# Products of ones on TensorE in a kernel of attention, eight experts and a feed-forward stage

## The chip, the cores and the metric

The kernel runs on one core of a Trainium2 chip. The metric is the device time of one execution in microseconds (us), from a few runs, of which the median is given. One further execution was profiled; its times are the rows shown below. The engines are TensorE (PE; its weight loads PEld), VectorE (DVE), ScalarE (ACT), GpSimd (POOL) and SyncE (SP), which issues DMAs. Each works through its own instructions in their order and waits for others by semaphores.

## The reference, cut to what matters

```python
scores = q @ k.T / sqrt(64) + cum[i] - cum[j]        # 32 heads, 576 rows, causal; cum = cumsum(log f)
x = softmax(scores) @ v                              # as 2304 tokens of 512
logits = normed(x) @ normed(expert_emb).T / tau      # 8 experts
e = argmax(logits); gate = softmax(logits)[e]
x = gate * (relu(x @ w1[e]) @ w2[e])                 # 512 -> 1024 -> 512, one expert for each token
h = x @ w_in
out = softplus(h) @ w_out                            # 512 -> 2048 -> 512
```

## The kernel before, in words

Nearly every product is split into a high and a low part so that float32 accuracy is kept: three products (high by high, high by low, low by high) stand where one would do.

**Attention** goes over 16 pairs of heads; a pair has five units (four blocks of 128 query rows, and one with the last 64 rows of both heads). One loop over n (80 units and some lags) writes the order of the work out by hand. In step n the letters of the string `NSTXVPXLXGLFAL` call in turn: N the normalising of an older unit, S the scores of unit n, X its softmax (DVE takes the maximum at L306, ACT the exponential), V the power of two that scales v (ACT squares at L249, POOL's `vmb` at L251, a product with ones on TensorE at L254, DVE's `vbits`), P the transposes of the next pair's q and k rows (`prep`, L207) and their split (ACT's copy, then POOL at L217 and L218), T and L the transposes of the probabilities and their split, A the product with v, F the transposes of finished rows (L454), G the logits. The loads of q, k, v and of the decay rows `cb` are issued on SP; `cb` can only be read back after `cum` has been computed and stored. PSUM has three banks for scores (tag s), three for transposes (T) and two for the products with v (A3, A2).

**Routing.** After the last logits DVE picks the expert of each row, TensorE counts ranks by products with a triangle of ones, and DVE computes counts, slots and tables: `pm(V)` (L781) makes, between other steps, the one-hot tables `pms[t]`, each 128x128, for 12 of the 20 row blocks (ACT makes the first eight). TensorE sums 20 products of them to `pid` (L835), from which comes the list of rows `gidx`. ACT meanwhile rounds the first expert's weights (L745, and at L1336 four tiles of its second matrix).

**Experts.** Nine phases, of three, two or one slot of 128 rows. POOL gathers a slot's rows (L1061), TensorE transposes them (L1085, for the first phase two at a time), ACT and DVE split them (L1086, L1087). Then eight groups of products `h` (L1149; in the first phase 12 products of 384 columns each), whose results leave through three PSUM banks: ACT's ReLU (`hh`, L1154) and DVE's rest (`hl`, L1155). Then the products `y` (L1129). In the first phase DVE splits four tiles of the second weight matrix (L1029) ahead of the first `hl`, and the gates (L861 to L870, root and exponential on ACT) are computed behind the first group. The weights of the next phases are loaded through four buffers (`raw`, SP), rounded on ACT and split on DVE into a ring of eight pairs of tiles, which TensorE frees.

**Feed-forward.** Five chunks of rows; products and softplus alternate until the end.

`g.onesm` is a tile of 128x128 ones in bfloat16, used later for sums over rows; POOL sets it at L82.

Of the kernel before, what the change touches and what calls it, by code (L numbers as in the profile page):

```python
# [9 lines left out]
F32 = mybir.dt.float32  # L10
# [14 lines left out]
B, H, S, D = 4, 8, 576, 64  # L25
N = B * S
DM = H * D
# [28 lines left out]
@with_exitstack  # L56
def body(ctx, tc, q, k, v, f, emb, tau, w1, w2, win, wout, out):
    nc = tc.nc
    const = ctx.enter_context(tc.tile_pool(name="const", bufs=1))
    dram = ctx.enter_context(tc.tile_pool(name="dram", bufs=1, space=DRAM))  # L60
    stage = ctx.enter_context(tc.tile_pool(name="stage", bufs=4))
    g = Shared()
    g.stage = stage
    g.xd = dram.tile([N, DM], F32, name="xd")
    g.gd = dram.tile([B * SB, 1], F32, name="gd")
    g.yd = nc.dram_tensor("yd", [N + 128 * NSLOT, WROW], F32, kind="Internal").ap()
    g.ydv = dram_disjoint_views(g.yd, NSLOT + 1)
    g.ncum = dram.tile([B * H, S], F32, name="ncum")

    nc.scalar.preload_act_table_set(LN_EXP)  # L70
    g.ident = const.tile([128, 128], F32, name="ident")
    make_identity(nc, g.ident)
    g.gidx = const.tile([128, NMAIN], I32, name="gidx")
    g.sidx = const.tile([128, NMAIN], I32, name="sidx")
    g.ids = const.tile([1, 3 * NG + 4], I32, name="ids")
    g.pv = const.tile([128, 3, NMAIN], F32, name="pv")
    g.gsl = const.tile([128, NMAIN], F32, name="gsl")
    g.tok = const.tile([128, NMAIN], F32, name="tok")
    g.grow = const.tile([128, NMAIN], I32, name="grow")
    g.oidx = const.tile([128, N // 128], I32, name="oidx")  # L80
    g.onesm = const.tile([128, 128], BF16, name="onesm")
    nc.gpsimd.memset(g.onesm, 1.0)  # L82
    g.ysq = const.tile([128, NSLOT], F32, name="ysq")
    nc.gpsimd.memset(g.ysq, 0.0)
    g.wsq = const.tile([128, 2, 8], F32, name="wsq")
    g.junk = const.tile([128, 1024], BF16, name="junk")
    g.lt = const.tile([128, T, E], F32, name="lt")
    g.mx = const.tile([128, T, 1], F32, name="mx")
    g.nrm = const.tile([128, T], F32, name="nrm")
    g.gs = const.tile([128, T], F32, name="gs")  # L90
    g.nr = const.tile([128, T, 1], F32, name="nr")

    const.tile([128, 40], F32, name="pad")
    g.const = const
    g.pre = []
    with ExitStack() as acc:
        ps_s = attention(tc, g, acc, q, k, v, f, emb, tau, w1)
        g.home = ctx.enter_context(tc.tile_pool(name="home", bufs=16, reuse_waits="tile"))
        ring = ctx.enter_context(tc.tile_pool(name="ring", bufs=8, reuse_waits="tile"))

        def wtile(dt=F32R, n=1024):
            return (ring.tile([128, n], dt, name="wh", tag="wh"), ring.tile([128, n], dt, name="wl", tag="wl"))

        g.wtile = wtile
        g.w2a = w2[0]
        with ExitStack() as rtx:
            route(tc, g, rtx.enter_context(tc.tile_pool(name="r_p", bufs=1)), ps_s)
    experts(tc, g, w1, w2, win, wout, out)


class Shared:
    pass


def attention(tc, g, acc, q, k, v, f, emb, tau, w1):
    nc = tc.nc
    ident, xd, ncum, nrm = g.ident, g.xd, g.ncum, g.nrm
    with ExitStack() as ctx:
# [5 lines left out]
        ps_s = acc.enter_context(tc.tile_pool(name="a_ps", bufs=3, space=PSUM))  # L124
        ps_t = acc.enter_context(tc.tile_pool(name="a_pt", bufs=3, space=PSUM))
        ps_a = acc.enter_context(tc.tile_pool(name="a_pa", bufs=1, space=PSUM))
# [21 lines left out]
        def load(i, what):  # L148
            r = loaded.setdefault(i, {})
            for nm in what:  # L150
                if nm == "v":
                    r[nm] = rows_in(vbuf[i % 3], v, i)
                elif nm == "c":
                    bh = 2 * i
                    c = r[nm] = ld.tile([128, 3, S], F32, name="cb", tag="cb")
                    for h in range(2):
                        nc.sync.dma_start(c[:, h], ncum[bh + h:bh + h + 1, :].to_broadcast([128, S]))
                        nc.sync.dma_start(c[64 * h:64 * h + 64, 2], ncum[bh + h:bh + h + 1, :].to_broadcast([64, S]))
                else:
                    r[nm] = rows_in(ld.tile([128, 5, 2, D], F32, name=nm + "t", tag=nm + "t"), q if nm == "q" else k, i)  # L160
# [373 lines left out]
        La, Lb, Lc, Lf, Lg = [2, 3, 4, 5, 8]  # L534
        seq = [(i, u) for i in range(NPAIR) for u in order]
        n_all = len(seq)
        prep(0, 0)
        nc.scalar.dma_start(ncum, cum)
        prep(0, 1)
        prep(0, 2)  # L540
        load(0, "c")
        load(1, "kvc")
        vs0 = scale(0)
# [23 lines left out]
        for n in range(n_all + Lg + 1):  # L567
            now = at_lag(0)
            if now and now[1] == order[0 if now[0] else 3] and now[0] + 2 < NPAIR:
                load(now[0] + 2, "qkcv")  # L570
            pt_ = ptrans(*at_lag(La)) if at_lag(La) else iter(())
            sf = soft(*now) if now else iter(())
            for c in "NSTXVPXLXGLFAL":
                if c == "S" and now:
                    scores(*now)
                if c == "N" and at_lag(Lc):
                    norm(*at_lag(Lc))
                if c in "TL":
                    next(pt_, None)
                if c == "X":  # L580
                    next(sf, None)
                if c == "A" and at_lag(Lb):
                    av(*at_lag(Lb))
                if c == "F" and at_lag(Lf):
                    for runs in ready(*at_lag(Lf)):
                        finish1(at_lag(Lf)[0], runs)
                if c == "G" and at_lag(Lg):
                    i, u = at_lag(Lg)
                    for runs in ready(i, u):
                        finish2(i, runs)  # L590
                    if u == order[-1] and i % 4 == 3:
                        pick(i // 4)
                        norms(i // 4)
                if c == "V" and now and now[0] + 1 < NPAIR:
                    steps = [order[x] for x in ([1, 2, 4] if now[0] else [2, 3, 4])]
                    if now[1] == steps[0]:
                        vsg = scale(now[0] + 1)
                    if now[1] in steps:
                        next(vsg, None)
                    if now[1] == order[4]:  # L600
                        vprep(now[0] + 1)
                if c == "P" and now:
                    for j, at_ in enumerate([0, 1, 3]):
                        if now[1] == order[at_] and now[0] + 1 < NPAIR:
                            prep(now[0] + 1, j)
            for x in (pt_, sf):
                for _ in x:
                    pass
            if n == 0:
                for _ in vs0:  # L610
                    pass
                vprep(0)
            if n == 6:
                gate_consts()
                pick_consts()
            if n == n_all - 20:
                for c in range(4):
                    r = g.stage.tile([128, 1024], F32, name="raw", tag="raw")
                    nc.sync.dma_start(r, w1[0, 128 * c:128 * c + 128, :])
                    g.pre.append(r)  # L620
            if n == n_all:
                rk = rank_start(tc, g, ps_s, oh)
# [107 lines left out]
def route(tc, g, p, psp):  # L730
    nc, lo, n, code = tc.nc, g.lo, g.n, g.code
# [8 lines left out]
    start = tl([128, T, NMAIN], "start", BF16)  # L740
# [17 lines left out]
    pms = [p.tile([128, 8, 128], BF16, name="pm", tag="pm", bufs=3) for _ in range(3)]  # L758
    first8 = pms[0]
    pms = [pms[t // 8][:, t % 8] for t in range(T)]  # L760
    made = iter(range(8, T))

    away = tl([128, 8, 128], "away", BF16)
# [13 lines left out]
    def pm(eng, k=1):  # L777
        for _ in range(k):
            t = next(made, None)
            if t is not None:  # L780
                eng.tensor_scalar(pms[t], g.iof, lo[:, t:t + 1], None, op0=ALU.is_equal)  # L781

    cnt = tl([128, 3, E], "cnt")
    r = tl([128, E], "r")
# [30 lines left out]
    x = 0  # L815
# [160 lines left out]
def experts(tc, g, w1, w2, win, wout, out):  # L976
    nc = tc.nc
# [5 lines left out]
    with ExitStack() as both, ExitStack() as ctx:  # L983
# [103 lines left out]
                nc.vector.tensor_sub(lo[:, cs, a], t, hi[:, cs, a].bitcast(F32))  # L1087

        def xprep(ph):
            for a in range(len(XG[ph])):  # L1090
                xslot(ph, a)

        def xnext(ph, turn):
            if ph + 1 < n_ph and turn < len(XG[ph + 1]):
# [236 lines left out]

        conv = Conv(tc, g, win, wout)
        xgather(0)
        for r in g.raw2:
            w = tuple(t.rearrange("p (a d) -> p a d", a=2) for t in g.wtile())
            nc.scalar.activation(w[0], r, ACTF.Copy)  # L1336
            g.first.append(w)
        TW = [(spare([128, 1024], F32R), spare([128, 1024], F32R)) for _ in range(4)]
        TR = [spare([128, 1024], F32) for _ in range(2)]
# [314 lines left out]
```

## Time and profile before

| | |
|---|---|
| median of 3 runs | 901.26 us (901.11 to 901.83) |
| profiled execution | 901.85 us, of which the span from first to last instruction is 900.1 us |
| mean granted TensorE clock | 0.983 |
| busy: PE, DVE, ACT, POOL | 857.4, 700.3, 565.7, 379.8 us |
| shares of the chain that ended last: PE, DVE, ACT, DMA | 71%, 11%, 5%, 4% |

How to read it: a timeline row has the start in us from the span's beginning, a duration in us, the engine, the line of the kernel, the operation with output<-input, sizes and the number of instructions merged, and in brackets how long the engine had been idle and what released it. [...] The chain follows the last instruction back to what released it at each step. The modelled end of a product includes its way through the array, so the distance of two starts is its cost, not the duration of one.

### The profile page before, as it was taken

To read this page: it belongs to the slowest core of one execution; us is meant where nothing else is said; L and a number is where in the kernel's file an instruction comes from. 1 tells how busy PE (TensorE), PEld (TensorE's weight loads), DVE (VectorE), ACT (ScalarE), POOL (GpSimd) and SP (SyncE) were. 2 spreads that over 40 slices of the span, in tenths; PEclk is the share of its full clock that TensorE was granted. 3 is DMA by queue.
4 is the path that set the end of the run, shared out by engine and by line. 5 is a ranking of instruction groups with operands and counts; after the bars stand their busy time and mean duration, and the time that the engine had idled before them with its cause. 6 is when DMAs were issued, how large, how long until landed. Compare 5 with 4: busy or idle time off the path is not lost.

```text
span 900.1 us, 17321 instructions
## 1 busy us (share of the span) xinstructions
PE 857.4 (95%) x6298; PEld 595.5 (66%) x6298; DVE 700.3 (78%) x1541; ACT 565.7 (63%) x1052; POOL 379.8 (42%) x524
## 2 busy tenths in 40 slices
PE   5999999999649999999899999999999999999998
PEld 4788787888549998998799744444444444664443
DVE  4888888888678777777689878778878787777775
ACT  5778879787554666674756775755445545566453
POOL 6678777767242222432513143325323322434221
PEclk9999999999759999999999999999999999999999
DMA  8967566681335888888868110102000100100001
GB/s 172 192 163 167 136 159 158 145 234 37 118 101 180 275 285 265 276 269 273 289 212 295 52 67 1 37 13 71 25 0 14 58 1 1 59 1 25 1 1 47
DMA packets 102816, 109.74 MB, mean 122 GB/s; under 512 B 62949, under 2 KB 72185, under 8 KB 102721
## 3 DMA queue, kind: packets, MB, share of 16 engines
q1 hardware_dynamic: 97282, 93.49, 36.9%
q0 software_dynamic: 5152, 14.87, 4.6%
q8 instruction: 52, 0.85, 0.4%
q14 instruction: 44, 0.35, 0.1%
q10 hardware_dynamic: 286, 0.17, 0.1%
HBM read 93.31 MB, written 15.20 MB: 121 GB/s over the span
## 4 chain that ended last, share of the span: by engine, by line
PE 71%; DVE 11%; ACT 5%; DMA 4%; POOL 4%; issue 4%; SPq 1%; DVEq 0%; POOLq 0%; ACTq 0%
PE h L1520 14%; PE h L1149 12%; PE y L1565 11%; PE y L1129 9%; PE t L1565 4%; PE s L284 4%; PE av L407 2%; PE pt L355 2%; POOL e L1534 2%; DVE r L1531 2%; DMA raw<-in_moe_w_dram 2%; DVE e L1545 2%; PE tps L207 1%; DVE wl L1041 1%; PE av L408 1%
## 5 line engine op out<-in xcount | busy, mean ns | idle before, releaser
L1534 POOL TENSOR_TENSOR e<-u,e 128x512 f32<-128x512 f32 (+1 forms) x80 | 105.2, 1316 | 240.4 <-DVE u L1533 237.1
L1530 ACT ACTIVATE e<-h,s_h 128x512 f32<-128x512 f32 (+1 forms) x80 | 51.2, 640 | 116.8 <-PE h L1520 116.8
L1565 PE MATMUL y<-dw,gh 128*128 128x512 f16 x448 | 111.4, 379 | 0.6 <-ACT ob L1573 0.6
L1552 DVE SCALAR_TENSOR_TENSOR gl<-e,s_gup,gh 128x512 f16<-128x512 f32 (+1 forms) x80 | 94.5, 1181 | 8.5 <-ACT gh L1550 8.1
L1565 PEld LDWEIGHTS <-gh 128*128 128x128 f16 x576 | 56.3, 98 | 65.2 <-issue 0.9
L1041 DVE TENSOR_TENSOR wl<-raw,wh 128x1024 fp32r<-128x1024 f32 x64 | 77.8, 1223 | 19.4 <-ACT wh L1040 19.3
L1149 PE MATMUL h<-xl,wh 128*128 128x384 f32 (+1 forms) x256 | 79.6, 311 | 1.7 <-DVE xl L1087 1.7
L1149 PE MATMUL h<-xh,wl 128*128 128x384 f32 (+1 forms) x256 | 79.7, 311 | 0.7 <-DVE wl L1041 0.5
L1040 ACT ACTIVATE wh<-raw 128x1024 fp32r<-128x1024 f32 x64 | 67.1, 1056 | 20.6 <-DMA raw<-in_moe_w_dram 19.2
L1149 PE MATMUL h<-xh,wh 128*128 128x384 f32 (+1 forms) x256 | 79.9, 312 | 0.0
L335 DVE SCALAR_TENSOR_TENSOR pts<-pt,pts 128x512 f16<-128x512 f32 (+3 forms) x128 | 69.9, 567 | 12.8 <-ACT pts L332 12.0
L1531 DVE TENSOR_SCALAR r<-h,s_h 128x512 f32<-128x512 f32 (+1 forms) x80 | 55.6, 695 | 31.1 <-ACT e L1530 31.1
L1520 PEld LDWEIGHTS <-wh 128*128 128x128 f16 x480 | 46.9, 98 | 46.7 <-issue 0.3
L1520 PEld LDWEIGHTS <-wl 128*128 128x128 f16 x480 | 47.0, 98 | 46.4
L1550 ACT ACTIVATE gh<-e,s_gup 128x512 f16<-128x512 f32 (+1 forms) x80 | 53.6, 671 | 36.1 <-DVE e L1546 36.1
L332 ACT ACTIVATE pts<-pt 128x512 f16<-128x512 f32 (+3 forms) x128 | 58.5, 495 | 22.7 <-PE pt L355 11.0
L309 ACT ACTIVATE p<-sm,mx 128x512 f32<-128x512 f32 (+3 forms) x128 | 67.8, 558 | 2.1 <-DVE mx L306 1.8
L1545 DVE TENSOR_TENSOR e<-r,e 128x512 f32<-128x512 f32 (+1 forms) x80 | 50.4, 630 | 22.4 <-POOL e L1534 22.4
L1129 PE MATMUL y<-wh,hh 128*128 128x512 f32 x168 | 67.8, 404 | 0.0
L306 DVE CUSTOM_DVE_ANT_0 sm<-s,cb 128x512 f32<-128x512 f32 (+3 forms) x128 | 58.3, 484 | 11.4 <-PE s L286 6.5
L1129 PE MATMUL y<-wl,hh 128*128 128x512 f32 x168 | 65.7, 391 | 0.0
L1520 PE MATMUL h<-yth,wh 128*128 128x512 f16 x192 | 64.9, 379 | 0.0
(344 smaller groups left out, 2421.5 us busy)
## 6 DMA issues: line engine op xcount, KB each, us to landing
raw<-in_moe_w_dram SPq DMA_DIRECT2D x68, 512.0 KB, 4.6
cb<-ncum SPq DMA_DIRECT2D x32, 288.0 KB, 4.7
raw<-in_moe_w_in_dram SPq DMA_DIRECT2D x16, 512.0 KB, 5.2
raw<-in_moe_w_out_dram SPq DMA_DIRECT2D x16, 512.0 KB, 5.2
yg<-yd SPq DMA_DIRECT2D x18, 264.0 KB, 2.8
cb<-ncum SPq DMA_DIRECT2D x32, 144.0 KB, 5.1
qt<-in_q_dram SPq DMA_DIRECT2D x32, 128.0 KB, 2.9
kt<-in_k_dram SPq DMA_DIRECT2D x32, 128.0 KB, 2.8
```

Source lines behind the costliest of these rows:

```text
L309: nc.scalar.activation(p[:, 0:n], s[:, 0:n], ACTF.Exp, scale=-1.0, bias=m)
L335: nc.vector.scalar_tensor_tensor(lo, ps, UP, hi, op0=ALU.mult, op1=ALU.subtract)
L1040: nc.scalar.activation(hi, r, ACTF.Copy)
L1041: nc.vector.tensor_sub(lo, r, hi.bitcast(F32))
L1129: nc.tensor.matmul(py[a], x[:, 128 * a:128 * a + 128], w[:, fb % 2], start=(fb == 0 and m == 0 and w is wh), stop=(fb == 7 and m == 1))
L1149: nc.tensor.matmul(pl, x[:, fs], y[:, c], start=(c == 0 and m == 0), stop=(c == 3 and m == 2))
L1520: nc.tensor.matmul(pl, w[:, fs], x[:, d], start=(d == 0 and m == 0), stop=(d == 3 and m == 2))
L1531: nc.vector.tensor_scalar(r, pl, back, 0.0, op0=ALU.mult, op1=ALU.max)
L1534: nc.gpsimd.tensor_sub(e, u, e)
L1545: nc.vector.tensor_sub(d, r, d)
L1552: nc.vector.scalar_tensor_tensor(gl, d, s, gh, op0=ALU.mult, op1=ALU.subtract)
L1565: nc.tensor.matmul(PO[c][a], x, w, start=(fb == 0 and m == 0 and w is wh), stop=(fb == FB - 1 and m == 1))
```

## The change

A helper issues products of a tile with another that write into a PSUM tile which nobody reads. It is called before the first transposes, between them, after the first unit's scaling, inside step 1 and after the last product with v, in the routing behind each of ten one-hot tables (with the table as weights), behind each of four rounded weight tiles (with the tile itself, 512 columns) and behind each of the first phase's three slots. The memset of `onesm` moves from POOL to DVE. The output is not touched.

```diff
@@ -79,7 +79,7 @@
     g.grow = const.tile([128, NMAIN], I32, name="grow")
     g.oidx = const.tile([128, N // 128], I32, name="oidx")
     g.onesm = const.tile([128, 128], BF16, name="onesm")
-    nc.gpsimd.memset(g.onesm, 1.0)
+    nc.vector.memset(g.onesm, 1.0)
     g.ysq = const.tile([128, NSLOT], F32, name="ysq")
     nc.gpsimd.memset(g.ysq, 0.0)
     g.wsq = const.tile([128, 2, 8], F32, name="wsq")
@@ -110,6 +110,11 @@
 
 class Shared:
     pass
+
+
+def spin(nc, ps, x, y, n):
+    for _ in range(n):
+        nc.tensor.matmul(ps[0:x.shape[-1], 0:y.shape[-1]], x, y, start=True, stop=True)
 
 
 def attention(tc, g, acc, q, k, v, f, emb, tau, w1):
@@ -534,10 +539,14 @@
         La, Lb, Lc, Lf, Lg = [2, 3, 4, 5, 8]
         seq = [(i, u) for i in range(NPAIR) for u in order]
         n_all = len(seq)
+        idle = ps_a.tile([128, 4 * (D + 1)], F32, name="av", tag="A2")
+        spin(nc, idle, g.onesm, g.onesm, 30)
         prep(0, 0)
         nc.scalar.dma_start(ncum, cum)
+        spin(nc, idle, g.onesm, g.onesm, 4)
         prep(0, 1)
         prep(0, 2)
+        spin(nc, idle, g.onesm, g.onesm, 3)
         load(0, "c")
         load(1, "kvc")
         vs0 = scale(0)
@@ -599,6 +608,8 @@
                         next(vsg, None)
                     if now[1] == order[4]:
                         vprep(now[0] + 1)
+                if c == "P" and n == 1:
+                    spin(nc, idle, g.onesm, g.onesm, 20)
                 if c == "P" and now:
                     for j, at_ in enumerate([0, 1, 3]):
                         if now[1] == order[at_] and now[0] + 1 < NPAIR:
@@ -610,6 +621,10 @@
                 for _ in vs0:
                     pass
                 vprep(0)
+                spin(nc, idle, g.onesm, g.onesm, 20)
+            if n == n_all + Lb - 1:
+                g.idle = ps_s.tile([128, 512], F32, name="idle", tag="s")
+                spin(nc, g.idle, g.onesm, g.onesm, 20)
             if n == 6:
                 gate_consts()
                 pick_consts()
@@ -758,6 +773,7 @@
     pms = [p.tile([128, 8, 128], BF16, name="pm", tag="pm", bufs=3) for _ in range(3)]
     first8 = pms[0]
     pms = [pms[t // 8][:, t % 8] for t in range(T)]
+    spin(nc, g.idle, g.onesm, g.onesm, 12)
     made = iter(range(8, T))
 
     away = tl([128, 8, 128], "away", BF16)
@@ -779,6 +795,8 @@
             t = next(made, None)
             if t is not None:
                 eng.tensor_scalar(pms[t], g.iof, lo[:, t:t + 1], None, op0=ALU.is_equal)
+                if k == 1:
+                    spin(nc, g.idle, pms[t], g.onesm, 3)
 
     cnt = tl([128, 3, E], "cnt")
     r = tl([128, E], "r")
@@ -1087,8 +1105,11 @@
                 nc.vector.tensor_sub(lo[:, cs, a], t, hi[:, cs, a].bitcast(F32))
 
         def xprep(ph):
+            idle = ps_y.tile([128, DM], F32, name="y", tag="y") if ph == 0 else None
             for a in range(len(XG[ph])):
                 xslot(ph, a)
+                if ph == 0:
+                    spin(nc, idle, g.onesm, g.onesm, 6)
 
         def xnext(ph, turn):
             if ph + 1 < n_ph and turn < len(XG[ph + 1]):
@@ -1331,9 +1352,11 @@
 
         conv = Conv(tc, g, win, wout)
         xgather(0)
+        idle = ps_y.tile([128, DM], F32, name="y", tag="y")
         for r in g.raw2:
             w = tuple(t.rearrange("p (a d) -> p a d", a=2) for t in g.wtile())
             nc.scalar.activation(w[0], r, ACTF.Copy)
+            spin(nc, idle, w[0][:, 0, 0:128], w[0][:, 0], 3)
             g.first.append(w)
         TW = [(spare([128, 1024], F32R), spare([128, 1024], F32R)) for _ in range(4)]
         TR = [spare([128, 1024], F32) for _ in range(2)]
```

## Rows read from the trace of the kernel before

**Rows 1.** The page: the granted clock in 40 slices of 22.5 us, in tenths.

```profile
PEclk9999999999759999999999999999999999999999
```

**Rows 2.** Windows: stretch, length, PE busy (instructions), granted clock, DMA share, GB/s.

```profile
...
237.00:238.00 1.00, 0.00 (x0) 0.90 0.00 0
...
268.00:269.00 1.00, 1.00 (x6) 0.74 0.97 381
...
```

**Rows 3.** The chain that ended last, from the third slot's rows on: start, us, what.

```profile
261.24 0.68 PE t L1085 x2
...
262.83 0.70 PE t L1085 x2
...
263.99 10.74 PE h L1149 x48
...
283.32 2.09 PE y L1129 x9
...
318.47 4.32 DMA raw<-in_moe_w_dram
```

**Rows 4.** Timeline of PE at the first loads.

```profile
4.47 1.09 PE L207 MATMUL tps<-ident,qt 128*128 128x128 f32 x4 [4.47 <-DMA qt<-in_q_dram]
...
17.25 1.09 PE L207 MATMUL tps<-ident,kt 128*128 128x128 f32 x4 [2.20 <-DMA kt<-in_k_dram]
...
27.76 0.60 PE L207 MATMUL tps<-ident,qt 128*128 128x128 f32 x4
```

**Rows 5.** Timeline of PE in the first phase, around the rise of the clock.

```profile
267.50 0.52 PE L1149 MATMUL h<-xl,wh 128*128 128x384 f32 x1
267.82 0.52 PE L1149 MATMUL h<-xh,wl 128*128 128x384 f32 x1
...
269.02 0.34 PE L1149 MATMUL h<-xl,wh 128*128 128x384 f32 x1
269.20 0.33 PE L1149 MATMUL h<-xh,wl 128*128 128x384 f32 x1
```

**Rows 6.** Timeline of POOL and DVE at the first loads.

```profile
1.26 0.19 POOL L82 MEMSET onesm<- 128x128 bf16 x1
...
13.07 0.69 DVE L306 CUSTOM_DVE_ANT_0 sm<-s,cb 128x512 f32<-128x512 f32 x1 [2.13 <-DMA cb<-ncum]
...
15.09 0.62 POOL L217 TENSOR_SCALAR qhi<-qraw 128x512 fp32r<-128x512 f32 x1 [4.79 <-ACT qraw L216]
...
21.55 1.28 POOL L218 TENSOR_TENSOR klo<-kraw,khi 128x512 fp32r<-128x512 f32 x1
...
23.15 0.19 POOL L251 TENSOR_SCALAR vmb<-vm 128x1 bf16<-128x1 f32 x1 [0.32 <-ACT vs L249]
```

**Rows 7.** Timeline of PE at the end of attention.

```profile
238.15 0.66 PE L454 MATMUL xt<-ident,xb 128*128 128x128 f32 x2 [1.56 <-DVE xb L429]
```

**Rows 8.** Timeline of DVE and PE in the routing.

```profile
247.45 0.25 DVE L781 TENSOR_SCALAR pm<-iof,lo 128x128 bf16<-128x128 bf16 x1
...
250.48 0.24 DVE L781 TENSOR_SCALAR pm<-iof,lo 128x128 bf16<-128x128 bf16 x1
...
252.00 1.23 PE L835 MATMUL pid<-rhs,pm 128*128 128x63 bf16 x20 [6.60 <-DVE rhs L829]
```

**Rows 9.** Timeline of ACT and PE between routing and first phase.

```profile
252.35 3.88 ACT L1336 ACTIVATE wh<-dw 128x1024 fp32r<-128x1024 f32 x4
...
258.47 1.09 PE L1085 MATMUL t<-ident,xg 128*128 128x128 f32 x4 [5.25 <-DMA xg<-xd,gidx]
```

**Rows 10.** Timeline of DVE in the first phase.

```profile
264.74 4.67 DVE L1029 TENSOR_TENSOR wl<-dw,wh 128x1024 fp32r<-128x1024 f32 x4
269.33 0.55 DVE L1155 SCALAR_TENSOR_TENSOR hl<-h,hh 128x384 fp32r<-128x384 f32 x1
270.48 0.18 DVE L863 TENSOR_SCALAR nr<-nr 128x20 f32<-128x20 f32 x1 [0.60 <-ACT nr L861]
...
280.01 1.01 DVE L1155 SCALAR_TENSOR_TENSOR hl<-h,hh 128x384 fp32r<-128x384 f32 x2
```

## The prediction

> **What bounds the kernel now.** I read the granted clock first. [...] The start was read as a timeline. There the clock line shows full speed, yet four transposes take 1.09 us at 4.47 and at 17.25 and 0.60 us at 27.76 [rows 4], so I take the first loads as slow. The products run at one column per cycle: 384 columns start 0.32 us apart at 267.5 and 0.18 us apart at 269.0 [rows 5]. From this the ones cost 128/384 of it, 0.107 us each slow and 0.06 fast, and a product of 512 columns 0.43 or 0.24.
>
> **The first loads.** Thirty ones are 3.2 us. The memset takes 0.19 us and stood on POOL at 1.26 behind others [rows 6]; on DVE it stands first, so the ones begin before 1.3 and end near 4.4, at about where the q rows land (4.47). DVE then only waits for its first load, so the moved memset costs nothing, and on POOL it frees 0.19 us that nobody waits for. If that cover were gone it would be 0.2 us. Four and three more (0.75 us) delay scores that nobody reads before 13.07, where DVE waits for cb [rows 6]. The first twenty lie ahead of scores whose banks that same DVE step must free. The second twenty (2.14 us) fit the wait of 2.20 us for kt at 17.25 [rows 4]. What comes back? TensorE's work after 17.25 could run up to twice as fast, but POOL holds the path: started by the copy that follows 13.07, it works from 15.09 to 22.83 and then waits 0.32 us for ACT before vmb [rows 6]. TensorE's next product needs vmb, so only that wait can go, less its signal: **0.25 us**, bounds 0 and 0.32. [...]
>
> **The end of attention.** Twenty ones behind the last sum (1.2 us at the fast level) cover the time up to 237.8, so the fall comes later and the two transposes at 238.15 (0.66 us [rows 7]) run fast. Four cost 1.09 or 0.60, so a pair saves 0.25. ACT and POOL behind them are the path: **0.25 us**, bounds 0 and 0.3. The ones end before the transposes' input is there.
>
> **The routing.** Twelve ones follow the ranks while DVE computes; ten groups of three (0.32 us a group) follow the one-hot tables that DVE makes from 247.45 to 250.7 [rows 8]. Slow, they end near 251.1, before pid's input at 252.00, and DVE is not asked to wait for them. The sum pid takes 1.23 us for 20 products; were the clock up, up to half of it would go. Before it TensorE has had only three microseconds of work, less than the 4.5 us of products (263.99 to 268.5) that stood before the one recorded rise, so I take **0**, bounds 0 and 0.6.
>
> **The weights and gathers.** Twelve products of 512 columns follow four ACT copies, 252.35 to 256.2 [rows 9]. Slow they take 5.1 us, 253.3 to 258.5; the first gathered rows' transposes start at 258.47. With pid this is 6.5 us of nearly unbroken products, so by the same row the clock should rise in it, near 256.5 to 258. Then six ones (0.36 fast) follow each of the three slots. The slots of the path are the second and third: pairs of 0.68 and 0.70 us [rows 3], each 0.25 cheaper. So the first product of h starts 0.5 us earlier; the last six ones may cost it 0.1 of that.
>
> **The first product, h.** Slow from 263.99 to 268.5 are 14 products; at 0.18 instead of 0.32 they save 1.96 us. TensorE alone would so gain 2.5. But its results leave through three banks that DVE must read, and DVE is late: four splits of weights from 264.74 hold it for 4.67 us, the first result is read at 269.33, then it waits 0.60 for the gates' root on ACT, and the fifth and sixth results are read from 280.01, 1.01 us for two [rows 10]. DVE starts 0.5 earlier, and the wait of 0.60 goes, because the first result, which ACT takes ahead of the root, is there two microseconds sooner. So the fifth result's bank is free at 280.5 - 1.1 = 279.4, the eighth group starts then and takes 12 x 0.18 = 2.16, until 281.6. Before it ended at 283.32 [rows 3]. **1.7 us**, bounds -0.35 (six slow ones in front of h, no faster clock) and 2.5. What is late next is DVE.
>
> **Does it last?** Behind 283 TensorE is the path for most of the time. Weight loads such as that from 318.47 (4.32 us [rows 3]) enter the chain, but their buffers are freed by splits that follow TensorE's results, so they start earlier too: no loss, bound 0.4.
>
> **Sum.** 0.25 + 0.25 + 1.7 = 2.2 us. The profiled run took 901.85 (span 900.1 and 1.75 around it), so 899.65. That run is 0.59 above the median of 901.26, against which it is **899.1**. What a measurement can tell from no change is 0.2%, 1.8 us. All upper bounds (0.32 + 0.3 + 0.6 + 2.5) make 3.7: 897.5.
>
> **Rivals.** *The clock falls again between the gathers.* Before, it fell at 237.8 although the sums had run until 1.2 us earlier (the row at 238.15 shows 1.56 of waiting [rows 7]), and 1.5 us lie between the last product on weights and the first slot, more between slots one and two. Then the transposes are slow, DVE starts no earlier, and h turns fast in its first microseconds: only the 0.60 goes, the eighth group ends at 282.1, gain 1.2, in all 1.7: 899.6. For it speaks that the slots leave TensorE idle more than half of the time. [...]
>
> *The change does not do what it says:* the ones come in too short pieces, the clock rises at 268.5 as before, and the six in front of h cost 0.35 slow. 0.25 and 0.25 stay: 0.15 in all, 901.1. Against it speak the 6.5 us from 252.00.
>
> *Slower:* the products stand in the way. TensorE works in order; should each cost twice its columns because its weights load first, thirty behind the tables need 6.4 us, pid starts 2.1 late, twelve on the weights need 10.3 and end near 265.6, and with three slots of 1.6 us behind them h starts near 270.9, 6.9 late. Its products would then all be fast (1.96) and 0.5 stays from before: about 905.7. It decides once a product of ones costs more than (252.00 - 247.7)/30 = 0.143 us. Against it: pid's 20 products of 63 columns, each with weights of its own, take 0.06 us each at the slow level.
>
> **How the numbers follow.** Forecast 0.47 (899.1, most of its spread above a gain of 1.8), the falling clock 0.23, no rise 0.21, products in the way 0.06, something unseen 0.03. Faster by over 0.2%: 0.85 of the first, half of the second, 0.52 in all; slower 0.07; the rest, 0.41, within it. The range takes the first three cases with the bounds: 897.5 to 901.4.
>
> **What would show it.** [...] Wrong: 0.32 between h's first products; pid or the first slot starting behind ones; a DVE that starts its one-hot tables later; a gain at 284 that is gone at 330.

## The result and the profile after

**Slower.** The changed kernel took 907.84 us (median of 6 runs, 904.49 to 911.03), the kernel before 901.20 beside it (6 runs, 900.67 to 901.83): a ratio of 1.0072 with a 95% interval of 1.0054 to 1.0090, 6.5 us. The prediction was 899.1, and its range ended at 901.4. The profiled execution is the fastest of the six: 904.49 us, span 902.7, mean granted clock 0.987 (before 0.983). So by the record the clock is up for longer, as intended, and the time is worse.

The page after: span, and the granted clock in 40 slices [rows 1].

```profile
span 902.7 us, 17659 instructions
...
PEclk8999999999979999999999999999999999999999
```

The dip of the routing has shrunk from two slices (7, 5) to one of 7, and the first slice now shows 8. By one-microsecond windows the granted clock was 0.50 of full speed for 23.9 us in place of 30.7 (before, the 0.90 of 237 to 238 and the 0.74 of 268 to 269 [rows 2] put it at 0.50 from 237.8 to 268.5), but in four pieces: 15.2 to 22.0, 243.9 to 250.7, 254.1 to 257.6 and 261.0 to 267.8.

Windows of PE after (columns as in [rows 2]).

```profile
243.00:244.00 1.00, 0.38 (x3) 0.95 1.17 215
...
254.00:255.00 1.00, 1.00 (x4) 0.57 0.06 16
...
260.00:261.00 1.00, 0.00 (x0) 0.99 0.65 225
...
267.00:268.00 1.00, 1.00 (x9) 0.60 0.42 164
```

The fall of 237.8 has moved to 243.9. After the routing's ones the clock is up at 251, falls again inside the products on the weights (0.57 in 254 to 255), and once more at 261.0, ahead of the transposes. It rises for good at 267.8, only 0.7 us sooner than before.

Timeline of PE after, from the end of attention to h [rows 5, 7 to 9].

```profile
238.66 0.41 PE L459 MATMUL xt<-ident,xb 128*128 128x128 f32 x2 [0.45 <-DVE xb L434]
...
248.11 3.31 PE L117 MATMUL idle<-onesm,pm 128*128 128x128 bf16 x30 [1.15 <-DVE cnt L811]
252.29 0.77 PE L853 MATMUL pid<-rhs,pm 128*128 128x63 bf16 x20 [0.88 <-DVE rhs L847]
253.71 4.62 PE L117 MATMUL y<-wh 128*128 128x512 f32 x12 [0.64 <-ACT wh L1358]
261.25 0.45 PE L1103 MATMUL t<-ident,xg 128*128 128x128 f32 x1 [2.92 <-PEq L1334]
263.73 0.90 PE L1103 MATMUL t<-ident,xg 128*128 128x128 f32 x3 [2.03 <-issue]
...
268.08 0.42 PE L1170 MATMUL h<-xh,wh 128*128 128x384 f32 x1
...
269.07 0.33 PE L1170 MATMUL h<-xl,wh 128*128 128x384 f32 x1
269.24 0.33 PE L1170 MATMUL h<-xh,wl 128*128 128x384 f32 x1
```

Down to 253.71 the kernel keeps its schedule: pid starts at 252.29 (before 252.00) and takes 0.77 in place of 1.23. Then the first slot's transposes, which started at 258.47 before [rows 9], start at 261.25: one of four, held by TensorE's own sequencer at L1334, and after 2.03 us more the other three. h starts 4.1 us late (268.08 against 263.99 [rows 3]), with its products 0.17 apart from the third on.

The chain of waits after, the same stretch [rows 3].

```profile
261.25 0.45 PE t L1103
261.70 2.03 issue
263.73 0.90 PE t L1103 x3
...
268.73 4.62 DVE wl L1047 x4
273.35 0.47 DVE hl L1176
...
283.64 2.38 PE h L1170 x12
286.02 2.09 PE y L1150 x9
```

"issue" stands in the chain: time in which TensorE waits for nothing that the profile shows. From h to y now takes 286.02 - 268.08 = 17.9 us in place of 283.32 - 263.99 = 19.3, with DVE in the chain, so 1.4 of the 4.1 comes back. The rest, 2.7, is there at the end: the spans differ by 2.6.

**What stands at L1334** (L1313 before) is `tails(...)`, called between the four rounded weight tiles and the first slot. It loads the count of rows over the fixed slots into a register and branches past a long body when that is zero, as here. Every engine has that branch in its order; here is TensorE's, which the profile puts under the sequencer of its weight loads.

The sequencer's rows of that line, first before, then after: duration in ns (least, median, most), first and last start.

```profile
L1313 PEldq EVENT_SEMAPHORE  x2: 51/51/51, 257.2 to 257.4; - x2
...
L1313 PEldq COMPARE_BRANCH  x1: 4267/4267/4267, 252.9 to 252.9; - x1
```

```profile
L1334 PEldq EVENT_SEMAPHORE  x2: 51/51/51, 260.9 to 261.0; - x2
...
L1334 PEldq COMPARE_BRANCH  x1: 3645/3645/3645, 257.1 to 257.1; - x1
```

Before, TensorE came to the branch at 252.9, right behind pid, and its 4.27 us ended at 257.2, inside the wait that [rows 9] shows as 5.25 us for the gathered rows. Now twelve products on the weights stand in front. The branch starts at 257.1, and its 3.65 us run until 260.8 with nothing beside them. The rows should be there by then: POOL issues the first gather at 254.43, where before one issued at 254.59 let the transposes start at 258.47.

### The profile page after: what moved, and what is told of

Same layout as the page of the kernel before. It is cut to its first block, busy times and chain, and to the rows that moved or that the text cites. A ratio compares the mean times of both kernels' runs of the same rounds, so it can differ in the third digit from the quotient of the medians.

```text
span 902.7 us, 17659 instructions
## 1 busy us (share of the span) xinstructions
PE 869.8 (96%) x6467; PEld 606.5 (67%) x6467; DVE 701.5 (78%) x1542; ACT 565.7 (63%) x1052; POOL 378.7 (42%) x523
## 4 chain that ended last, share of the span: by engine, by line
PE 51%; DVE 10%; ACT 3%; POOL 3%; issue 3%; DMA 1%; DVEq 0%; POOLq 0%; ACTq 0%
PE h L1543 14%; PE y L1588 11%; PE h L1170 10%; PE y L1150 9%; PE t L1588 4%; POOL e L1557 2%; DVE r L1554 2%; DVE e L1568 2%; DMA raw<-in_moe_w_dram 1%; DVE wl L1059 1%; PE t L1103 1%; ACT wh L1058 1%; DVE e L1569 1%; DVE dw L1461 1%; DVE u L1556 1%
## 5 line engine op out<-in xcount | busy, mean ns | idle before, releaser
L1059 DVE TENSOR_TENSOR wl<-raw,wh 128x1024 fp32r<-128x1024 f32 x64 | 77.8, 1223 | 18.7 <-ACT wh L1058 17.9
```

The lines of the kernel that those rows point to most:

```text
L1059: nc.vector.tensor_sub(lo, r, hi.bitcast(F32))
```

## The experiments

Two theories stood first. **Branch** (A in the expectations): the products on the weights push the branch out of its cover. **Clock** (B): the falls inside the gathers, or what the ones do to the first loads, cost the time. Letters from C on stand for later theories, which each expectation spells out. The three kinds of products (first loads, routing and slots, weights) can be taken out one by one. Each ratio is to the kernel before, timed on the same chip, with its 95% interval in brackets. A product that is left out is always one that nobody reads.

**The change again**, unaltered, to see whether the effect repeats.

> The changed kernel once more, for its spread and for a second trace. Theory A (TensorE reaches the branch ahead of the overflow tails behind the products on weights, at 257.1 instead of 252.9, and the 3.6 us that the branch takes are no longer hidden): 904 to 911 us, every run late, the branch again between 256 and 259, the first product of h behind 267. Rival B (the clock alone: low stretches at other places than before): the time goes with the low stretches, about half a microsecond for each one of them, and the branch plays no part.

1.0065 [1.0045, 1.0085], 906.90 us (903.85 to 909.66). The effect repeats. In its trace the single transpose stands at 260.61, the other three after 3.00 us of "issue" at 263.91, and h at 268.35.

**Without the products on the weights.**

```diff
-        idle = ps_y.tile([128, DM], F32, name="y", tag="y")
...
-            spin(nc, idle, w[0][:, 0, 0:128], w[0][:, 0], 3)
```

> The twelve products on weights taken out, all other ones left. A: the branch is reached at about 253 and its wait is hidden behind the gather again; first product of h by 264.5; 899 to 901.5 us, and the spread shrinks. B: the spread and most of the loss stay, 904 us or more.

1.0007 [0.9993, 1.0021], 902.59 us. Most of the loss is gone, but not all, and the runs spread from 898.79 to 905.18. The profiled one was the slowest, and it shows a second loss, ahead of the routing.

Windows of PE at the first loads, without the products on the weights.

```profile
20.00:22.00 2.00, 0.66 (x6) 1.00 1.07 266
22.00:24.00 2.00, 0.88 (x11) 0.69 1.31 193
24.00:26.00 2.00, 2.00 (x27) 0.50 0.95 180
26.00:28.00 2.00, 2.00 (x18) 0.50 0.75 227
28.00:30.00 2.00, 2.00 (x12) 0.60 1.20 209
```

Timeline of PE, POOL and DVE in the same execution.

```profile
20.24 0.42 PE L350 MATMUL pt<-ident,p 128*128 128x128 f32 x2
22.87 0.19 POOL L256 TENSOR_SCALAR vmb<-vm 128x1 bf16<-128x1 f32 x1
23.12 0.16 PE L259 MATMUL vb<-vmb,onesb 128*128 128x1 bf16 x1 [2.46 <-DMA qt<-in_q_dram]
...
252.18 0.25 DVE L797 TENSOR_SCALAR pm<-iof,lo 128x128 bf16<-128x128 bf16 x1
```

With the clock up, TensorE has done its work by 20.7 and waits 2.46 us until POOL's `vmb` lets the product at 23.12 go. (The row names a load of q rows as the releaser. But `vmb` ends at 23.06, 0.06 before the product, and in the kernel before, the change and its repeat the product starts 0.05 or 0.06 behind `vmb` too.) In that wait, at 22.8, the clock falls, and until 29.6 TensorE works almost without a gap at a granted clock of 0.50 (which comes again in this execution from 39.8 to 43.2). The first one-hot table comes at 252.18; before it came at 247.45 [rows 8].

The timed runs bear it out, since each comes with its mean granted clock. Here the seven at 0.983 or less took 901.8 to 905.2 us (median 903.9), the five at 0.984 or more 898.8 to 902.0 (median 899.8). In the changed kernel the clock goes from 0.987 (904.49) down to 0.979 (911.03), nearly in the order of the times. Its profiled execution was one that did not fall at 23.

The traces with ones at the first loads agree on the price. Where the clock is never slow between 22 and 44, the first table comes at 247.71 (the change), 247.13 (its repeat), and 247.34 and 246.35 (the wait filled, below). With 3.4 us at the slow level there it comes at 249.42 (the first loads alone, below) and 249.34 (the change with 64 unexecuted products, below), and with 10.2 us at 252.18 (here) and 252.04 (the weights behind the branch, below): about half of the slow time is lost.

**The products on the weights alone**, added to the kernel before (the helper, its tile and the line removed above).

> The kernel before with the twelve products on weights alone. A: branch at 257 to 258.5, first product of h at 267.5 to 269; if the clock is then up, its products save some 2 us of that: 903 to 906 us. B: within 1 us of the kernel before.

1.0018 [1.0009, 1.0027], 903.08 us (901.73 to 903.78), a narrow spread.

Timeline of PE, then the sequencer's row of the branch, products on the weights alone.

```profile
261.37 0.94 PE L1090 MATMUL t<-ident,xg 128*128 128x128 f32 x4 [2.62 <-PEq L1318]
...
265.66 0.69 PE L1154 MATMUL h<-xh,wh 128*128 128x384 f32 x1
```

```profile
L1318 PEldq COMPARE_BRANCH  x1: 3816/3816/3816, 257.1 to 257.1; - x1
```

The branch starts at 257.1 as in the changed kernel, the transposes follow it at 261.37, and h is 1.7 us late (265.66, where the expectation had 267.5 or more). But all four transposes come together: the gap of 2 to 3 us behind the first is not there, and the loss is 1.6 us, not 6.5. Two losses were left to find.

**The products on the weights behind the branch**, all else as changed.

```diff
-            spin(nc, idle, w[0][:, 0, 0:128], w[0][:, 0], 3)
...
         tails(nc.values_load(ids[0:1, 3 * NG + 3:3 * NG + 4], min_val=0, max_val=3 * NG,
                              skip_runtime_bounds_check_because="a sum of counts"))
+        for w in g.first[4:]:
+            spin(nc, idle, w[0][:, 0, 0:128], w[0][:, 0], 3)
         xprep(0)
```

> The twelve products on weights moved behind the branch, ahead of the first slot's transposes. A: the branch starts at 253 as before and ends near 257.2; the products then hold TensorE until 260 (fast) or 262.5 (slow), the first slot waits for them: first product of h at 264 to 266.5, 900 to 903.5 us. B: the same as the changed kernel, 904 to 911 us.

1.0026 [1.0013, 1.0038], 903.50 us (900.85 to 907.01). Better than the change, worse than leaving them out: the twelve run from 261.38 for 4.61 us, and the transposes start at 265.83. By an estimate the rows were there near 263.2: their gather is issued at 259.18, and without the products one issued at 259.32 let the transposes start at 263.30. So twelve are too many for what is left of the wait behind the branch. This execution, too, fell between 22 and 30, and its first table came at 252.04.

**Neither the first loads nor the weights** (routing, end of attention and slots alone).

> Only the ones of the routing and of the slots are left. Theory C (two causes: the branch that is reached late behind the products on weights, and a clock that falls at 23 because TensorE, made fast by the ones of the first loads, runs out of work before POOL's vmb): neither cause is left. Attention ends as before, the first product of h comes by 263.5, 899 to 900.8 us, no run above 902.8. Rival D (any products that nobody reads shift the clock's falls about and so spread the times): a spread of 5 us or more, up to 905.

0.9988 [0.9979, 0.9997], 899.00 us (898.26 to 901.84). This part of the change pays, by a little over a microsecond.

**The first loads alone** (30, 4, 3, 20 and 20 ones and the memset on DVE).

> Only the ones of the first loads. C: two groups of runs, one at 900.5 to 902 and one 3 to 5 us later, whose trace has the granted clock at 0.50 between 23 and 30; the branch at 253 in the first. D: one broad group, not tied to a low stretch between 23 and 44.

1.0030 [1.0016, 1.0043], 903.19 us (900.07 to 906.66).

Windows of PE at the first loads, these ones alone.

```profile
22.00:24.00 2.00, 0.96 (x21) 0.98 1.30 197
24.00:26.00 2.00, 2.00 (x20) 0.50 0.95 209
26.00:28.00 2.00, 2.00 (x18) 0.67 0.98 266
```

The fall is there without any other part (at 23.9, 0.9 us behind the end of the wait for `vmb`, which took 2.75 us), and the first table comes at 249.42. So the first loads lose 2.7 us by themselves. The runs don't form the two groups that theory C expected: they spread evenly, as D had it, while the trace shows the low stretch of C.

**All but the first loads.**

> All but the ones of the first loads: weights, routing, slots. C: the branch is late as in the changed kernel, attention is not: 902.5 to 905 us in one group no wider than 3 us. D: as wide as the changed kernel, up to 910.

1.0008 [0.9999, 1.0017], 901.17 us (900.38 to 901.86). That is below the 902.5 to 905 that theory C expected. The difference to the run with neither the first loads nor the weights (0.9988), +0.0020, is what the weights cost (+0.0018 alone). But with +0.0030 for the first loads the sum is 1.0038, and the change measures 1.0072 and 1.0065. About 3 us are missing, the size of the gap after the first transpose; in this trace all four come together at 260.63. What differs here is where the code lies: 77 products fewer stand in front of the branch's target.

**End of attention and routing alone.**

> Only the ones at the end of attention and in the routing. C: pid and the last transposes of attention are fast, the branch is reached a little earlier than before, h as slow as before at its start: 900 to 901.2 us. If the ones of the slots are what makes h fast, 0.5 to 1.5 us more than without weights and first loads; if they cost, less.

0.9999 [0.9990, 1.0008], 900.03 us (899.17 to 903.00). pid takes 0.77, but h starts slow at 262.10 and stays so until 267: alone it buys nothing, since the clock falls again in the gathers. That the slots' ones make the difference to 0.9988 is likely and not shown, since the two intervals overlap.

**Does the place of the code matter?** The 77 products go back into the kernel without the first loads, but inside the body that is skipped. They never run; they only put what follows back to where it lies in the changed kernel. In the changed kernel itself 64 such products (63 and 1) move it further on, away from there.

```diff
             with tc.If(over > 0):
+                pads = [bank(), bank()]
+                spin(nc, pads[0], g.onesm, g.onesm, 76)
+                spin(nc, pads[1], g.onesm, g.onesm, 1)
```

> As the run without the ones of the first loads, with 77 products put into the branch that is skipped (they are never executed): what stands behind the branch comes to lie where it lies in the changed kernel. Theory E (after the branch the code comes in pieces, and where the target lies late in a piece TensorE gets one transpose and waits 2 to 3 us for the next piece): the one transpose and the gap of 2 to 3 us of the changed kernel are back, 902.5 to 904 us. Rival F (the gap belongs to the ones of the first loads or to a gather that lands late): no gap, 901.2 us as without the products.

> The changed kernel with 64 products in the skipped branch. E: the target lies in another place of its piece, all four transposes of the first slot come together, 2 to 3 us less than the changed kernel: 903.5 to 905 us in the median, with the spread of the first loads left. F: 906 to 908 us.

77 products that never run cost about 3 us: 1.0041 [1.0025, 1.0056], 904.04 us (903.16 to 906.23), against 1.0008 without them.

Timeline of PE: first without the 77, then with them.

```profile
260.63 0.63 PE L1096 MATMUL t<-ident,xg 128*128 128x128 f32 x4 [3.52 <-PEq L1327]
```

```profile
263.04 1.12 PE L1096 MATMUL t<-ident,xg 128*128 128x128 f32 x4 [5.38 <-issue]
```

The sequencer's rows with the 77.

```profile
L1327 PEldq EVENT_SEMAPHORE  x2: 51/51/51, 259.7 to 259.9; - x2
...
L1327 PEldq COMPARE_BRANCH  x1: 3446/3446/3446, 256.2 to 256.2; - x1
```

The branch is no later than without them (256.2 against 256.4) and is over by 259.7, yet the transposes start at 263.04, 3.1 us after the last thing the sequencer did there. The first loads are not in this kernel, so they are not the cause. Nor is the gather, which is issued at 253.50: POOL comes to its branch behind it at 254.7, earlier than without the 77 (255.4).

The profile's DMA view adds something. It lists a queue q8 that carries instructions, in packets of 16 KB (52 packets, 0.85 MB in the kernel before). One of them starts at 253.88 in the kernel before and one at 258.13 in the change, each 1.0 us behind the start of TensorE's branch (252.9 and 257.1). With the 77 one passes at 260.8, inside the standstill, and one more at 264.3, 1.3 us behind its end. In the change one passes at 261.5, and the next at 265.1, 1.3 us behind the end of its standstill at 263.73. Without the 77 one passes at 261.0, with the transposes running since 260.63, and none follows up to 266, where that view ends. So the standstill may end where TensorE goes over to the next piece of code: that is inferred from these times. No row says that it waited for that piece.

The other way round: 1.0045 [1.0029, 1.0060], 905.20 us (900.68 to 907.46), and the gap is gone.

Timeline of PE, the change with 64 unexecuted products.

```profile
262.79 1.09 PE L1103 MATMUL t<-ident,xg 128*128 128x128 f32 x4 [2.71 <-PEq L1334]
```

The branch ends at 262.4, and four transposes follow together. That execution fell at 23.5 (first table 249.34), which is why its rows are late. The median is just above theory E's range, and its interval touches those of the change, so of this run the row is the evidence rather than the ratio.

**Filling the wait at 21**, on the first loads alone: 36 ones ahead of the product that waits for `vmb`.

```diff
+                if c == "V" and n == 3:
+                    spin(nc, idle, g.onesm, g.onesm, 36)
```

> As the run with the ones of the first loads alone, with 36 more ahead of the second product with vmb, where TensorE had waited 2.5 us for POOL in the traces in which the clock fell at 23. Theory C (the idle time before vmb lets the clock fall, and the work behind it then takes twice as long): no low stretch between 23 and 30, the runs above 903 are gone: 900 to 902 us, somewhat later where the clock was slow at 20 anyway. Rival D: the same spread, 900 to 907.

> The filled wait before vmb once more, for the two of twelve runs that stayed above 903. C: in a late run the clock falls at another wait of the first 45 us, and one in six or fewer are late; the median stays within 1 us of the kernel before. D: a third or more late, median above 902.

1.0005 [0.9990, 1.0021], 900.65 us (899.59 to 906.09), and on another chip 1.0010 [0.9998, 1.0022], 901.23 (899.34 to 904.64): from 1.0030 nearly back to 1.

Timeline of PE, the wait filled.

```profile
20.31 2.17 PE L117 MATMUL av<-onesm 128*128 128x128 bf16 x36
...
23.48 0.16 PE L259 MATMUL vb<-vmb,onesb 128*128 128x1 bf16 x1 [0.99 <-DMA qt<-in_q_dram]
```

Neither trace falls at 23. In each series two runs stay above 903; with 0.976 to 0.979 they have the lowest clocks but for one run at 0.977, so the fall seems rarer and not gone. Whether those runs fell at 23 no trace shows. And the repeat of the change waited 2.50 us there without falling: the fall came in or just behind a long wait there, but not behind every one. What decides is open.

**A better version.** Without the first loads, the products on the weights behind the branch, but fewer of them: two for each tile, then one.

```diff
+        for w in g.first[4:]:
+            spin(nc, idle, w[0][:, 0, 0:128], w[0][:, 0], 1)
         xprep(0)
```

> No ones at the first loads; two instead of three products on each weight tile, and behind the branch instead of ahead of it; routing and slots as in the change. Theory A (only what stands ahead of the branch is late): the branch at 252 to 253, the eight products run beside the wait for the gathered rows, the first product of h at 263 to 264 and fast: 897.5 to 899.5 us, below the run without weights. Rival: the products push the first slot back and nothing is gained, 899 to 901.

> The ones of the routing and the slots alone, once more on whatever chip it gets. Theory C: neither late branch nor early fall, 0.5 to 2 us below the kernel before, and no second group of runs. Rival G (its first result was the luck of one layout or chip): within 0.4 us of the kernel before, or above it.

> No ones at the first loads, one product on each weight tile behind the branch, routing and slots as in the change. The four products end by 258, so unlike the eight they do not push the first slot. A: the first slot's transposes at 257.5 to 258.5, the first product of h at 262.5 to 263.5, and 0.5 to 1.5 us below the eight products' 900.2; if the clock is not up in h, the same as routing and slots alone.

Eight: 0.9994 [0.9985, 1.0003], 900.18 us; they end later than the rows land and push the first slot to 259.70, as the rival had it. None (the kernel of 0.9988, on another chip): 0.9984 [0.9975, 0.9993], 899.13 us. Four: 0.9980 [0.9970, 0.9990], 898.71 us (898.19 to 900.22).

Timeline of PE, four products behind the branch.

```profile
256.17 2.04 PE L117 MATMUL y<-wh 128*128 128x512 f32 x4 [3.41 <-PEq L1327]
258.02 1.09 PE L1096 MATMUL t<-ident,xg 128*128 128x128 f32 x4
...
262.76 0.44 PE L1163 MATMUL h<-xh,wh 128*128 128x384 f32 x1
```

The branch is covered again, the four fill what was left of the wait for the rows, and the transposes start at 258.02, close to the 258.47 of before. h starts at 262.76; its first three products start 0.46 and 0.28 apart, the later ones 0.17. This beats both kernels, the one before by 2.1 us and the changed one by about 8 (by the ratios, 0.9980 against 1.0072 and 1.0065). That it beats the version with no products on the weights, 0.4 us behind it, is not shown: the difference is inside the intervals.

## Why the prediction was wrong

Three things went wrong: a wait that was taken as free and was not, the place of the code, and the first loads. What the ones were to gain elsewhere came in the main.

**The weights and gathers: the step that failed first.** "Slow they take 5.1 us, 253.3 to 258.5; the first gathered rows' transposes start at 258.47", and so they were costed at nothing. The products themselves were sized well: twelve start at 253.71 and take 4.62. The cover was misread. [Rows 9] says that TensorE sat idle for 5.25 us and that a DMA ended it. It doesn't say that the sequencer was free: the branch ran from 252.9 to 257.2, so nearly 4 us of that wait were its own. Pushed 4.2 us back (252.9 to 257.1), the branch became the path, for 1.6 to 1.8 us. What becomes late next was asked of DVE ("What is late next is DVE"), not of TensorE's own queue, where the sequencer's rows of the trace of before showed it.

**The place of the code was not in the sum at all.** Every added product moves what is behind it. By the runs with unexecuted products the place alone is worth 3.0 us (1.0041 - 1.0008, of 900 us). Why a place costs time is not shown. That the gap is the loading of the next piece of code is inferred from the times of the packets alone (265.1 behind a gap that ended at 263.73, 264.3 behind one that ended at 263.04). The runs show only that the place decides (1.0008 without the 77, 1.0041 with them), and the rows that "issue" stands in the gap: no engine, semaphore or transfer of data is named as waited for.

**The first loads.** The bounds were 0 and 0.32, a loss excluded. Its pieces were right: ones of 0.11 us (thirty in 3.38) and POOL the path. `vmb` came at 23.24 in the profiled execution, whose clock was slow until 22, and at 22.85, 22.87 and 23.07 in three traces whose clock was up at 20; 23.15 [rows 6] less the term of 0.25 is 22.9. But the product behind `vmb` comes anywhere from 22.86 to 23.59 in the traces without these ones, so a gain of 0.25 is neither shown nor excluded. What was missing is what a faster TensorE does when another engine sets the pace: it waits longer, here 2.46 to 2.86 us in five traces with these ones and the clock up, against 0.28 before. The 2.5 us so opened lie right in front of a stretch in which TensorE works without a gap, and where it did so at 0.50 for 10.2 us, the first one-hot table came 4.3 to 5.8 us later (252.04 and 252.18 against 246.35 to 247.71). The term of 0.25 gained was 2.7 lost (1.0030). That the wait is the cause rests on the filled runs (1.0005 and 1.0010); why the clock falls behind it in some executions and not in others stays open.

**What held.** The products cost by their columns: at full speed in the kernel before those of 256 start 0.12 us apart and those of 384 0.17, against 0.32 at a granted clock of 0.50, which is 1.8 times as long and not twice. At the end of attention the pair of transposes took 0.41 for 0.66, the 0.25 predicted. pid was taken as 0 with a bound of 0.6 and saved 0.46 in this execution; in others, such as that with 252.18, it took 1.23. From h's first product to y, 1.4 us were saved where the term, less the earlier start of 0.5, was 1.2, with DVE the releaser. No gain was lost after 283: the 2.7 us lost there stay to the end. The routing, the end of attention and the slots alone gave 1.1 and 1.4 us in two series, and 2.1 with four products on the weights behind the branch, where 1.95 (the sum without the first loads) was forecast.

**The rivals.** The granted clock did fall to 0.50 between the gathers, as the first said (261.0 to 267.8, transposes at 1.12 us for four). The slower one had the right sign and place, TensorE's order ahead of the gathers, and the wrong mechanism: the thirty products on the tables, for which it had 6.4 us, took 3.31, 0.11 us each, so it did not decide.

**The new sum**, in parts of the time before: routing and slots -0.0012 to -0.0016, weights ahead of the branch +0.0020, the place of the code +0.0033, first loads +0.0030. Together +0.0067 to +0.0071, against 1.0065 and 1.0072 measured. Each term is uncertain by about 0.001, so the agreement is closer than the runs can vouch for.

## What to carry to other kernels

Before work is put into an engine's wait, read the sequencer's rows of that wait as well as its releaser: here a branch used nearly 4 of the 5.25 us already, and the work belonged behind it. Where an engine is sped up ahead of a slower one, look at what its new idle time does: here the wait for `vmb` went from 0.28 to between 2.46 and 2.86 us, and the granted clock fell in it or up to 0.9 us behind it in four of five traces. And added instructions move all the code behind them, here at a cost of 3.0 us; where a branch lands, the same edit with unexecuted instructions tells the cost of the place from the cost of the work.

## What was not expected of the hardware

A branch over a skipped body takes 3.4 to 4.3 us on TensorE in these traces, against 50 to 72 ns in the rows of the other engines. Behind its target TensorE stood still for another 2.0 to 3.1 us in three traces, after one transpose in the change and in its repeat, and before any with the 77; 77 products that are never executed bring it about and 64 others take it away. And extra work lowered the granted clock: with ones at the first loads alone the runs' mean is 0.975 to 0.981, and the three longest runs have 0.975 to 0.977. Part of the distance to 0.982 to 0.985 before is a stretch of the first loads that was recorded as full speed there [rows 1, 4].
